# A scan, attention-like blocks and a two-layer GELU network on one core: weight quarters loaded in turns, decay rows in four blocks, a new order of steps

## The chip, the cores and the metric

The kernel runs on one core of one Trainium2 chip. The metric is the device time of one execution in microseconds; three runs were made, and the median counts. All times below that are not called a run's are from one profiled execution, counted from the start of its span. The engines are PE (matmuls; its weight loads are shown as PEld), DVE (VectorE), ACT (ScalarE), POOL (GpSimd) and SP, which issues DMAs here.

## The reference

The first part is a linear recurrence over the sequence, in chunks (a state space model), for 4 batches, 8 heads, 768 positions, 32 channels (D) and a state of 16 (N). The second part is a two-layer network on the 3072 rows of 256 that come out:

```python
log_a = np.log(np.clip(a, 1e-06, 1.0))
for c in range(nc):                       # chunks of 32
    cum = np.cumsum(la, axis=-1)
    L = np.exp(cum[..., :, None] - cum[..., None, :]) * causal
    M = np.einsum('bhin,bhjn->bhij', Cc, Bc) * L
    y = einsum('bhij,bhjd->bhid', M, xc) + einsum('bhin,bhnd->bhid', Cc, state) * np.exp(cum)
    state = exp(sum(la)) * state + sum over j of B_j x_j * exp(cum_last - cum_j)
...
h = y_rows @ w_in                         # 3072 x 256 by 256 x 2048
g = 0.5 * h * (1.0 + np.tanh(c * (h + 0.044715 * h * h * h)))
out = g @ w_out                           # 2048 x 256
```

## The kernel before, in words

**Tiles.** The kernel takes chunks of 128 positions: 6 a batch, 24 in all. Two chunks are a unit, so there are 12 units of 256 rows. The decay factors are products of `a` within a chunk; they are put into B and C (`mul`: C divided by, B multiplied with the factor), so that the block of weights of a chunk is a masked product of C and B.

**Steps of a unit u.** `G.u` multiplies C and B of the unit's two chunks into four PSUM banks (`ga` and `gb` are two each; 8 short matmuls); `M.u.0` and `M.u.1` (DVE) mask the two halves with the triangle and write them out as bf16. `D.u` makes the chunk's own addition to the state, `S.u.k` adds it to the old state, `SP.c` spreads the state of chunk c over heads. `Y.u` multiplies masked weights with x and C with the old state into the bank `yb`, and `yev.u` copies that into `xm`, the input of the network. `s1.u.i` (8 a unit, 4 matmuls of 256 columns each, L717) is the first layer, into one of two PSUM buffers `hp`; `gelu.u.i` (ACT, L721) empties it into `gT`. `s2.c.q` (4 a chunk, 4 matmuls of 256 columns, L735) is the second layer, summed over q in a bank `o_ps` (or, near the end, `yb`), emptied by `oev.c` and written out by `store.c`. Step q of `s2` needs GELUs 2q and 2q+1 and quarter q of w_out.

**Batch 0** is done in a shorter way. Its first four chunks have their own rows of a (`load_aq`, `clipq`, `Rq` the scan, `tpq` the transpose, `recip0`), and `mulc`, `mulb`, `tw` (transposes on PE), `ew` (their copies out of PSUM). x comes in by `load_x4`, is cast by `x4.k` (tile `x4b`), and `XX.u` and `XD.u` bring it into order and form the state's addition on PE; `xn.c` copies it out. Chunks 4 and 5 have `mul1`, `T1`, `ce1`, `bh1`, `N1`, `bn1`. For unit 0, `GE.2`, `GE.3` (ACT) and `ME.2`, `ME.3` (POOL) do the second half of M.

**Other batches.** `load_bc.b.i` brings in C and B. Batch 1 turns them on PE (`T.1.i`, copies `E.1.i`, then `F.1`, `N.1`, `bn.1`); batches 2 and 3 by a scratch tensor in DRAM and a transposing DMA (`load_wr`, `load_tr`, `load_bn`). `castx.u` casts x of units 2 and on. The decay factors of all batches come from two blocks of 32 rows with half a sequence each, `a_t` [64, 384]: `clip`, `R` (scan), then `tp6.0` to `tp6.3` and `tp2` (four calls) turn them by 32 rows at a time, `recip` and `recip1` invert, and `pe`, `pp`, `pend` make the factor of a whole chunk.

**Weights.** w_in and w_out come in as four quarters each (`load_wi.q`, `load_wo.q`, 512 KB, tile `wf`) and are cast in halves (`wi.q.k`, `wo.q.k`) by POOL, ACT or DVE.

**The order.** The string `ORDERED` lists all steps by hand; a step is recorded when its name comes up, on its own engine or on the one named behind the colon (`:D`, `:A`, `:P`). Each engine works through its list in order, and semaphores make it wait for data and for a buffer to be free. `~n` is n blocks of 128 columns of filler matmuls on zeros (into `yb`), `+10` is such filler ahead of an `s1` step; they are no part of the result. All large loads are issued by SP, the rows of `a` in part by ACT. A DMA that uses the same completion counter as the one eight places earlier waits for that one to land. The pools that matter: two buffers `hp`, one `o_ps`, one `yb`, eight for weight quarters, six for x.

```python
ORDERED = """
load_aq.0 load_aq.1 load_aq.2 load_aq.3 c_wz load_bc0.1 c_ident c_m4 c_sel c_tri c_zero load_bc0.0
c_unp load_a.0:A clipq load_x4 Rq tpq recip0 c_cz mulc.0 ~59 tw.1 load_wi.0 c_warm load_a.1:A
...
"""
```

Of the kernel before, what the change touches and what calls it, by code (L numbers as in the profile page):

```python
# [8 lines left out]
FP32 = mybir.dt.float32  # L9
# [8 lines left out]
load_aq.0 load_aq.1 load_aq.2 load_aq.3 c_wz load_bc0.1 c_ident c_m4 c_sel c_tri c_zero load_bc0.0  # L18
c_unp load_a.0:A clipq load_x4 Rq tpq recip0 c_cz mulc.0 ~59 tw.1 load_wi.0 c_warm load_a.1:A
ew.1.1:A mulc.1 c_bmask c_m8 tw.2 mulb ~4 tw.0 peq ew.0.2:A clip ew.0.1 load_wi.1 ew.0.0:A ew.1.2  # L20
c_par ~2 G.0 x4.1 ew.1.0 M.0.0 ~1 ppq GE.2 pendq x4.0:P XX.0 ME.2 XD.0 GE.3 xn.1 ME.3 xn.0:D
load_wi.2 SP.0 ~17 Y.0 wi.0.1:A wi.0.0:A S.0.0 yev.0.0.2 wi.1.1 XX.1 wi.1.0:A R XD.1 S.0.1
load_wi.3 S.1.0 s1.0.0 SP.1 xn.2 load_bc1.1 wi.2.0 gelu.0.0 G.1 s1.0.1 s1.0.2 M.1.1 M.1.0
load_bc1.0 load_wo.0 wi.3.0:D gelu.0.1 wi.2.1 s1.0.3 load_x.2 SP.2 pe wi.3.1 gelu.0.2 load_bc.1.1
gelu.0.3 tp6.2 s1.0.4 load_bc.1.0 gelu.0.4 load_x.3 load_wo.1 xn.3 s1.0.5 s1.0.6 Y.1 gelu.0.5 pp
tp2 gelu.0.6 tp6.3 recip1 s1.0.7 S.1.1 yev.1.0.2 mul1.0:P mul1.1:P tp6.1 pend gelu.0.7 s1.1.0
wo.0.1 T1.0 s1.1.1 T1.1 gelu.1.0 bh1 N1 gelu.1.1 s1.1.2 tp6.0 s1.1.3+10 bn1 ce1.1 load_wo.2
castx.2.None SP.3 wo.0.0 ce1.0 gelu.1.2 gelu.1.3 G.2 s1.1.4 recip.1.4 s1.1.5 gelu.1.4 M.2.1
mul.1.1:P s2.0.0.0.o D.2 M.2.0 load_x.4 gelu.1.5 s2.0.1.0.o s1.1.6 T.1.1 gelu.1.6 S.2.0 s1.1.7
SP.4 Y.2 mul.1.0 yev.2.0.2:D gelu.1.7 wo.1.0 wo.1.1 T.1.0 E.1.1:A castx.3.None:A s1.2.0 wo.2.0  # L30
s1.2.1 E.1.0 wo.2.1 load_wo.3 load_bc.2.1 N.1 gelu.2.0 F.1 s1.2.2 bn.1:D G.3 gelu.2.1 gelu.2.2 D.3
s1.2.3 s2.0.0.1.o S.3.0 S.3.1 load_bc.2.0 gelu.2.3 s1.2.4 M.3.1 s2.0.1.1.o s1.2.5 SP.6 gelu.2.4
s1.2.6 M.3.0 gelu.2.5 wo.3.0:D gelu.2.6 s2.0.0.2.o castx.4.None s1.2.7 Y.3 gelu.2.7 wo.3.1:D
s2.0.1.2.o S.4.0 yev.3.0.2 S.4.1 s2.0.0.3.o oev.0 load_x.5 s1.3.0 s1.3.1 mul.2.1 s2.0.1.3.o
load_wr.2.1 load_x.6 gelu.3.0 gelu.3.1 s1.3.2 oev.1:D SP.8 s1.3.3 s2.1.0.0.o gelu.3.2 M.4.0
# [50 lines left out]
def kernel(  # L86
# [14 lines left out]
    Q = 128  # L101
# [882 lines left out]
```

## Time and profile before

| | |
|---|---|
| runs | 118.29 us median of 3 (118.04 to 118.46) |
| the profiled execution | span 116.9 us; its own time outside of the span isn't recorded, and the median run is 1.4 us above the span |
| busy in the span | PE 110.1 (94%), ACT 72.1 (62%), DVE 69.4 (59%), POOL 21.4 (18%) |
| matmuls of the first layer (L717) | 384, 53.3 us of rows; 4 of them are issued in 0.437 us |
| matmuls of the second layer (L735) | 384 in two groups, 47.3 and 4.6 us of rows, at the same pace |
| GELU (L721, ACT) | 96, 596 ns each |
| first L717, last L735 | 12.50, 113.87 us |
| DMA | 16 MB; queue busy nearly all the time to 32 us |
| granted TensorE clock | 1.00 throughout |

Rows of PE overlap: a matmul's row lasts longer than the step to the next matmul. What it costs is the step, so the chain that ended last, which counts only steps, gives 0.437 us for four matmuls of 256 columns. In a row of the timeline the first number is the start, the second how long the group lasted, and the bracket at the end is the idle time before it with what ended that. A DMA's issue row is not its transfer; the list of DMA issues gives the time from issue to landing. In the chain, PE has 75% of the span, and DMA and SP's queue 14%, these two all before 16.7 us.

### The profile page before, as it was taken

What the parts mean: (1) busy time and instruction counts of PE and PEld (TensorE: products, weight loads), DVE (VectorE), ACT (ScalarE), POOL (GpSimd) and SP (SyncE); (2) the same over time, 40 slices, a digit from 0 to 9 for tenths busy, and PEclk for the clock granted to TensorE, in tenths of its full rate; (3) what the DMA queues carried; (4) which work ended last, traced back from release to release, by engine and by line L of the source; (5) the groups of instructions that cost most, each with busy time, mean ns of one, the idle gap of its engine ahead of it and who ended that gap; (6) DMA issues with size and microseconds to landing.
All of it is one profiled execution on the core that took longest, in us unless ns stands there. A gap on an engine that the chain in (4) does not pass through costs nothing.

```text
span 116.9 us, 3379 instructions
## 1 busy us (share of the span) xinstructions
PE 110.1 (94%) x1426; PEld 92.0 (79%) x1426; DVE 69.4 (59%) x140; ACT 72.1 (62%) x139; POOL 21.4 (18%) x38
## 2 busy tenths in 40 slices
PE   6988999998899999999999999999999999999990
PEld 2354676776789979989898999889798998999970
DVE  5898899899785936716695583049493462101020
ACT  2249899968486459565766677828465587447501
POOL 7606816908206000052200000000000000000000
PEclk9999999999999999999999999999999999999999
DMA  0999997999983929998407472044201201101113
GB/s 26 228 332 357 281 252 178 208 288 257 305 143 90 185 47 219 213 253 200 72 25 171 121 163 63 0 140 98 40 6 63 71 0 52 43 0 50 45 47 132
DMA packets 43007, 15.97 MB, mean 137 GB/s; under 512 B 36657, under 2 KB 41457, under 8 KB 42993
## 3 DMA queue, kind: packets, MB, share of 16 engines
q1 hardware_dynamic: 42800, 15.64, 56.0%
q8 instruction: 11, 0.18, 0.6%
q10 hardware_dynamic: 192, 0.13, 0.5%
q14 instruction: 4, 0.02, 0.1%
HBM read 11.04 MB, written 3.93 MB: 128 GB/s over the span
## 4 chain that ended last, share of the span: by engine, by line
PE 75%; DMA 8%; DVE 6%; SPq 6%; issue 2%; POOL 1%; ACT 0%; DVEq 0%; POOLq 0%
PE o_ps L735 33%; PE hp L717 30%; DMA bcf<-in_B_dram 8%; PE yb L735 3%; SPq L190 3%; PE ga L603 3%; PE yb L658 2%; DVE m L613 2%; PE yb L667 2%; DVE ce L523 1%; SPq L150 1%; DVE bh L327 1%; DVE bc L484 1%; SPq L159 1%; SPq L183 1%
## 5 line engine op out<-in xcount | busy, mean ns | idle before, releaser
L721 ACT ACTIVATE gT<-hp 128x512 bf16<-128x512 f32 x96 | 54.3, 596 | 25.0 <-PE hp L717 24.6
L717 PE MATMUL hp<-xm,w_in_sb 128*128 128x256 bf16 x384 | 53.3, 273 | 0.6 <-ACT gT L721 0.4
L735 PE MATMUL o_ps<-w_out_sb,gT 128*128 128x256 bf16 x352 | 47.3, 273 | 0.0
L717 PEld LDWEIGHTS <-w_in_sb 128*128 128x128 bf16 x384 | 41.4, 114 | 3.5 <-issue 1.9
L735 PEld LDWEIGHTS <-gT 128*128 128x128 bf16 x384 | 37.0, 98 | 4.9 <-issue 1.1
L327 DVE COPY o_sb<-o_ps 128x256 f32<-128x256 f32 x13 | 5.5, 425 | 23.8 <-PE o_ps L735 20.4
L613 DVE TENSOR_TENSOR m<-ga,tri 128x1024 bf16<-128x1024 f32 x12 | 14.6, 1218 | 0.1
L613 DVE TENSOR_TENSOR m<-gb,tri 128x1024 bf16<-128x1024 f32 x11 | 13.4, 1219 | 0.7 <-PE gb L603 0.7
L323 ACT ACTIVATE o_sb<-o_ps 128x256 f32<-128x256 f32 x9 | 3.5, 385 | 9.2 <-PE o_ps L735 9.2
L705 PE MATMUL yb<-wz 128*128 128x512 bf16 (+3 forms) x23 | 7.6, 481 | 1.1 <-DVE wz L220 1.1
L691 DVE SCALAR_TENSOR_TENSOR sp_new<-s_new,pend,bmask 128x256 bf16<-128x256 f32 x17 | 7.9, 476 | 0.0
L327 DVE CAST xm<-yb 128x512 bf16<-128x512 f32 x6 | 4.1, 687 | 5.8 <-PE hp L636 4.8
L684 DVE SCALAR_TENSOR_TENSOR s_new<-s_new,pend,hp 128x64 f32<-128x64 f32 x13 | 3.6, 279 | 6.4 <-PE hp L636 6.2
L705 PEld LDWEIGHTS <-wz 128*128 128x128 bf16 x26 | 3.0, 120 | 5.1 <-issue 3.2
L667 PE MATMUL yb<-m,x 128*32 128x128 bf16 x192 | 6.1, 220 | 0.0
L603 PE MATMUL ga<-ce,bh 32*128 32x256 bf16 x48 | 4.7, 273 | 1.3 <-DVE bn L327 0.9
L484 POOL TENSOR_TENSOR bc<-bc_t,pt 128x768 bf16<-128x768 f32 x2 | 3.0, 1494 | 13.8 <-DMA bc_t<-in_C_dram 13.7
L658 PE MATMUL yb<-ce,sp_new 128*32 128x128 bf16 x160 | 5.3, 221 | 0.0
L603 PE MATMUL gb<-ce,bh 32*128 32x256 bf16 x48 | 4.7, 273 | 0.0
L735 PE MATMUL yb<-w_out_sb,gT 128*128 128x256 bf16 x32 | 4.6, 273 | 0.0
L667 PEld LDWEIGHTS <-x 128*32 128x32 bf16 x192 | 3.8, 97 | 0.8 <-issue 0.8
L323 ACT ACTIVATE xm<-yb 128x512 bf16<-128x512 f32 x6 | 3.6, 595 | 1.1 <-PE hp L636 1.1
(115 smaller groups left out, 79.5 us busy)
## 6 DMA issues: line engine op xcount, KB each, us to landing
out_dram<-o_sb SPq DMA_DIRECT2D x24, 128.0 KB, 1.9
x_t<-in_x_dram SPq DMA_DIRECT2D x20, 128.0 KB, 3.9
wf<-in_moe_w_in_dram SPq DMA_DIRECT2D x4, 512.0 KB, 6.7
wf<-in_moe_w_out_dram SPq DMA_DIRECT2D x4, 512.0 KB, 5.5
bc_t<-in_C_dram SPq DMA_DIRECT2D x3, 384.0 KB, 5.8
bc_t<-in_B_dram SPq DMA_DIRECT2D x3, 384.0 KB, 5.5
scr<-bc SPq DMA_DIRECT2D x4, 192.0 KB, 2.2
x_t<-in_x_dram SPq DMA_DIRECT2D x1, 512.0 KB, 5.8
```

Source lines behind the costliest of these rows:

```text
L323: nc.scalar.activation(o, i, AF.Copy)
L327: nc.vector.tensor_copy(out=o, in_=i)
L484: (nc.gpsimd if eng == "POOL" else nc.vector).tensor_tensor(out=d["bc16"][:, i], in0=d["bc"].rearrange("p i h (r n) -> p i r h n", r=R6)[: ...
L603: nc.tensor.matmul(out=gbank(g)[:, 256 * k:256 * k + 256], lhsT=bh_of(2 * u + k)[gs], rhs=ce_of(2 * u + k)[gs], start=True, stop=True, til ...
L613: nc.vector.tensor_tensor(out=m_of(u)[:, 2 * i:2 * i + 2].rearrange("p g k e t -> p (g k e) t"), in0=gx[i].rearrange("p g (k t) -> p (g k) ...
L658: nc.tensor.matmul(out=y4[32 * j:32 * j + 32, k, w], lhsT=sp[:, 32 * h:32 * h + 32], rhs=ce_of(gc)[:, h % 2], start=first(j), stop=False, ...
L667: nc.tensor.matmul(out=y4[32 * j:32 * j + 32, k, w], lhsT=X16[u][:, k, 32 * h:32 * h + 32], rhs=m[:, h // 2, h % 2, :], start=first(j), st ...
L691: nc.vector.scalar_tensor_tensor(out=sp_new.rearrange("p (g d) -> p g d", g=4), in0=(XN[0][:, H * D:H * D + 64] if gc == 0 else state[("s" ...
L705: nc.tensor.matmul(out=t[:, 0:m * 128], lhsT=wz, rhs=w3.to_broadcast([128, m, 128]), start=True, stop=True, skip_group_check=True)
L717: nc.tensor.matmul(out=hp[:, j * T:(j + 1) * T], lhsT=w_in_k[:, w, q, k], rhs=xm[:, w, u * T:(u + 1) * T], start=(w == 0), stop=(w == 1))
L721: nc.scalar.activation(gts[u][:, 2 * i:2 * i + 2], hps.pop((u, i)).rearrange("p (j t) -> p j t", j=2), AF.Gelu_apprx_tanh)
L735: nc.tensor.matmul(out=ops[gc], lhsT=gts[u][:, fi, k * Q:(k + 1) * Q], rhs=w_out_sb[:, fi, :], start=(fi == 0 and (u > 0 or k == 0)), stop ...
```

## The change

The order of steps is new throughout. What else changes:

- **Loads.** `load_aq` is one DMA of 128 rows in place of four. `a_t` has 128 partitions: four blocks of 32 rows, each with a quarter of the sequence (192 columns) and, beside it, rows for chunks 4 and 5; `load_a` are four DMAs, all issued by ACT. `load_x.u.k` are the two halves of `load_x.u`. SP's order of loads begins now: C, B, wi.1, x4, wi.0, wo.0, bc1 (B), wi.2, bc1 (C), wi.3, wo.1, half of x.2, wo.2, the other half, B and C of batch 1, wo.3, x.3, x.4.
- **Decay rows.** `tp6` is one transpose of [128, 192] and `tp2` one of [128, 64]; `recip.b` is one step for each batch. `pe` and `pend` fit the new layout (`pend` is two copies).
- **Constants.** Parts of `c_zero`, `c_sel` and `c_unp` become steps of their own (`c_az`, `c_ends`, `c_unz`, `c_selp`, `c_sub`); in the new order `c_selp` and `c_unp` are on POOL. `c_warm`, a GELU of one column, stands behind `oev.23`.
- **Start.** `mulb` and `x4` are cut into 2 and 4 pieces. `M` of unit 0 becomes `M.0.0`, `MD.0.3` (DVE, one bank), `GE.0.2` and `ME.0.2`; unit 1 has `M.1.0`, `GE.1.2`, `GE.1.3`, `ME.1.2`, `ME.1.3`. `XX.1` and `XD.1` go into the bank pair `gb`. `G.1` stands ahead of `XD.0`, and `XD.1` behind `s1.0.1`. `Y.0` and `yev.0` are done in two halves (`Yw.0.w`).
- **Second layer of units 0 and 1.** Both chunks of a unit are done by quarters in turn, side by side in one bank: unit 0 in `o_ps` (as before), unit 1 in `yb`.

```diff
-    def load_x(u):
+    def load_x(u, k):
...
-    def load_aq(i, eng):
-        (nc.scalar if eng == "ACT" else nc.sync).dma_start(out=aq_t[32 * i:32 * i + 32], in_=a_rows(i * Q, Q))
+    def load_aq(eng):
+        dma(eng)(out=aq_t, in_=a_of(0, Q, 4, batch * H, Q))
...
+        if i == 0:
+            dma(eng)(out=a_t[0:k, 0:2 * Q], in_=a_of(0, QL, 3, batch * H, 2 * Q))
+        elif i == 1:
+            dma(eng)(out=a_t[k:, 0:QL], in_=a_of(3 * QL, 0, 1, batch * H, QL))
+        elif i == 2:
+            dma(eng)(out=a_t[0:k, 2 * Q:AL], in_=a_of(4 * Q, Q // 2, 3, batch * H, Q))
+        else:
+            dma(eng)(out=a_t[k:, 2 * Q:2 * Q + Q // 2], in_=a_of(S - Q // 2, 0, 1, batch * H, Q // 2))
...
     def f_tp2():
-        for k in range(4):
-            turn(rt0[1][32 * k:32 * k + 32], r_t[32:64, Q + 64 * k:Q + 64 * k + 64], 2)
+        turn(rt0[1], r_t[:, 2 * Q:2 * Q + Q // 2], 2)
...
-    def f_tp6(q):
-        i, j = divmod(q, 2)
-        turn(rt[32 * q:32 * q + 32], r_t[32 * i:32 * i + 32, 192 * j:192 * j + 192], R6)
+    def f_tp6():
+        turn(rt, r_t[:, 0:QL], R6)
...
-            XN[c] = pso.tile([128, 512], FP32, name="o_ps") if c in (0, 3) else psh.tile([128, 512], FP32, name="hp")
+            XN[c] = gx[1][:, k] if u else pso.tile([128, 512], FP32, name="o_ps") if k == 0 else psh.tile([128, 512], FP32, name="hp")
...
+    def f_MD(u, g):
+        nc.vector.tensor_tensor(out=m_of(u)[:, g].rearrange("p k e t -> p (k e) t"),
+                                in0=gbank(g).rearrange("p (k t) -> p k t", t=Q), in1=tri_b(4), op=ALU.mult)
...
-            if u == 0:
+            if u < 2:
                 if k == 0:
-                    ops["0"] = pso.tile([128, 512], FP32, name="o_ps")
-                ops[gc] = ops["0"][:, k * d_model:(k + 1) * d_model]
+                    ops["u"] = yb if u else pso.tile([128, 512], FP32, name="o_ps")
+                ops[gc] = ops["u"][:, k * d_model:(k + 1) * d_model]
...
-        for k, q in [(k, q) for q in range(4) for k in range(2)] if u == 0 else [(k, q) for k in range(2) for q in range(4)]:
+        for k, q in [(k, q) for q in range(4) for k in range(2)] if u < 2 else [(k, q) for k in range(2) for q in range(4)]:
```

The new order, from the first `G` to the first steps of unit 2, and its last line:

```
tw.0 ew.0.0:A ew.0.2:D ew.1.0:A ~6 G.0 R
ew.1.2 ew.1.1:A c_tri c_selp:P wi.1.0 GE.0.2 c_unp:P ~3 ppq x4.2:P load_wo.0 x4.1:P pendq x4.0 M.0.0
MD.0.3 x4.3 ME.0.2 load_bc1.0 ~23 XX.0 wi.1.1:D c_par load_wi.2 wi.0.0 pe xn.1 G.1 XD.0 GE.1.2 tp2
xn.0:D SP.0 wo.0.0 pp S.0.0 ~4 Yw.0.0 Yw.0.1 GE.1.3 wi.0.1:D yev.0.1.2 mul1.0:P S.0.1 pend
load_bc1.1 wo.0.1 XX.1 yev.0.0.1:D load_wi.3 xn.3 wi.2.1 M.1.0 s1.0.0 s1.0.1 load_wo.1 gelu.0.0
load_x.2.0 XD.1 T1.0 wi.2.0 ME.1.2 load_wo.2 S.1.0 s1.0.2 recip1 ME.1.3:D gelu.0.1 s1.0.3 mul1.1 bh1
N1 xn.2 s2.0.0.0.o S.1.1 T1.1 SP.1 SP.2 wi.3.1 ce1.1:D SP.3 load_x.2.1 gelu.0.2 s2.0.1.0.o gelu.0.3
s1.0.4 ce1.0:D wi.3.0:D s1.0.5 bn1 Y.1 gelu.0.4 G.2 wo.1.0 tp6 wo.1.1:D s1.0.6 gelu.0.5 load_bc.1.0
s1.0.7 yev.1.0.2 M.2.1 gelu.0.6 s2.0.0.1.o s2.0.1.1.o gelu.0.7 s1.1.0 s1.1.1 wo.2.1:A M.2.0 gelu.1.0
gelu.1.1 wo.2.0 s2.0.0.2.o s2.0.1.2.o castx.2.None:D D.2 s1.1.2 recip.1 S.2.0 load_bc.1.1 SP.4
...
s2.11.1.1.o store.22 s2.11.1.2.o s2.11.1.3.o oev.23 c_warm store.23
```

More of the change, by code (lines that the diff above doesn't have):

```diff
@@ L30 @@
[L30 to L35, printed above, removed]
```

318 lines of the change are left out of this document (179 added, 139 removed).

## The prediction

> **What bounds the kernel now.** I read the table of stages (busy time of each engine in stretches of the span) first, then the chain that ended last, then the timeline from 2 to 34 us.
>
> ```profile
> core 0: us, PE busy (x) PEld busy (x) DVE busy (x) ACT busy (x) POOL busy (x), PEclk, DMA share, GB/s
> 12.00:16.00 4.00, 3.56 (x65) 2.52 (x62) 3.55 (x7) 3.50 (x8) 2.62 (x4) 1.00 1.05 261
> ...
> 24.00:28.00 4.00, 3.71 (x67) 3.05 (x66) 3.96 (x7) 2.86 (x5) 1.50 (x3) 1.00 1.02 303
> 28.00:32.00 4.00, 3.11 (x43) 2.57 (x41) 3.29 (x7) 2.10 (x5) 1.57 (x3) 1.00 1.10 290
> 32.00:36.00 4.00, 4.00 (x71) 3.42 (x69) 3.62 (x7) 2.77 (x6) 0.72 (x1) 1.00 0.67 119
> 36.00:60.00 24.00, 24.00 (x327) 21.36 (x325) 14.70 (x27) 15.31 (x29) 4.01 (x4) 1.00 0.78 155
> ```
>
> PE has no idle time left from 32 us on, to the end of the matmuls at 113.9; the DMA queue is busy throughout until 32. So the end is set by when PE starts its main work and by what it loses before 32 us. The chain is matmuls one after the other from 30.26 to 113.87 (83.6 us). Before that come the losses:
>
> ```profile
> 12.50 0.60 PE L717 MATMUL hp<-xm,w_in_sb 128*128 128x256 bf16 x4
> 14.67 1.09 PE L717 MATMUL hp<-xm,w_in_sb 128*128 128x256 bf16 x8 [0.20 <-ACT gT L721]
> 15.95 1.09 PE L717 MATMUL hp<-xm,w_in_sb 128*128 128x256 bf16 x8 [0.20 <-ACT gT L721]
> 29.69 0.28 PE L603 MATMUL ga<-ce,bh 32*128 32x256 bf16 x2 [0.89 <-DVE bn L327]
> ```
>
> From 12.5 PE has only first-stage matmuls, and alternates with the GELU over two banks: two groups (0.87 us of issue) every 1.28 us. The second stage cannot fill in, because its weights come late (the wo quarters land at 18.2, 26.2, 27.6 and 30.8). Later it waits for batch 1's tiles on DVE.
>
> The ledger of 12.50 to 30.26 (17.76 us) in issue times of the chain: 19 first-stage groups and 2 second-stage ones of 4 matmuls at 0.437 (9.18); G.1 to G.3 at 0.33 (0.99); Y.1, Y.2 at 0.56 (1.12); the transposes T1, N1 (0.66) and T.1, N.1 (1.05); pp, D.2, D.3 (0.52). That is 13.5, so 4.25 us are idle or filler (`s1.1.3+10`). This is all that the change can win after the first s1.
>
> **Part 1: the start.** The first s1 follows XX.0, XD.0, xn.0, SP.0, Y.0, yev.0, and XX.0 follows the load of x.
>
> ```profile
> 8.65 0.63 ACT L323 ACTIVATE x4b<-x_t 128x512 bf16<-128x512 f32 x1 [0.30 <-DMA x_t<-in_x_dram]
> 8.69 0.61 POOL L325 CAST x4b<-x_t 128x512 bf16<-128x512 f32 x1 [3.53 <-DMA x_t<-in_x_dram]
> ...
> 9.35 0.27 PE L571 MATMUL o_ps<-x4b,unp 32*128 32x256 bf16 x1 [0.48 <-POOL x4b L325]
> ```
>
> The a rows come in one DMA, C and B are issued at 0.81 instead of 1.73, and the constants leave DVE (POOL copies selp and unp). DVE started clipq at 4.25 though the rows had landed at 3.24, so the decay chain moves ahead by about 1 us, and G.0 from 8.13 to about 7.6, since it now also waits for half of mulb on POOL. None of it counts while XX.0 waits for x; without that cover it would be worth the 0.5 us of G.0. SP issues wi.1 before x4. With the landings of before (C 3.5 us after issue, B 1.14 later, 512 KB of w_in 1.42, x4 2.2) C lands at 4.35, B at 5.5, wi.1 at 6.9, x4 at 9.1 (8.63 before). The casts take 0.6 to 0.7 on POOL and ACT. POOL's queue before them now holds some 13 more short instructions and wi.1.0, and I put its end at 9.2 to 9.6: its memsets and copies go by the rows from 0.81 to 5.16 (0.2 to 0.9 each), and one cast is stretched as w_in's was beside the scan (1.04 against 0.61). XX.0 then starts at 10.0 to 10.2, 0.75 later. XD.0 now stands behind G.1 (0.33) and behind xn.1, which ACT must read out of the same bank: 11.2 to 11.5. Then xn.0 (0.34), SP.0 (0.4), Y (0.45), and on DVE S.0.0, wi.0.1 (0.42) and S.0.1 before yev's half (0.35). First s1 at **13.5, against 12.50: +1.0**. Bounds: +0.7 if POOL keeps up, +1.8 if the scan (0.94) stops it for its whole length.
>
> **Part 2: a second table load on ACT.** The new order has c_warm, the first GELU, at its end. The list of ACT's instructions then shows a table load before the first copy, which is free, and a second one between xn.3 and gelu.0.0.
>
> ```profile
> 2.21 1.28 ACT L231 ACT_TABLE_LOAD   x1 [2.21 <-issue]
> ...
> 3.50 0.20 ACT L231 ACTIVATE warm<-warm 128x1 f32<-128x1 f32 x1
> ```
>
> xn.3 (after XX.1) ends at 13.8, the load at 15.1; without it gelu.0.0 would start at 14.2, when s1.0.0 is through. PE meanwhile does s1.0.0, s1.0.1, XD.1 (0.38), T1.0 (0.22) until 15.0, then waits for the bank of gelu.0.0 until 15.7: 0.7 us lost. I take the row's 1.28.
>
> **Part 3: PE from there.** In the new order quarters of s2.0, XD.1, T1 and N1 stand between the s1 groups, so that PE no longer waits for GELUs (0.49 apart): from 15.1 to 32 ACT has 19 GELUs and 7 other pieces, 12.4 of 17 us. Whether the quarters are there in time goes by the queue, with the same increments (bc1 1.2, wo 1.5, x 0.5 a half, bc_t 2.1). Landing, then ready after its cast or multiply, then PE's need by issue times in order:
> wi.2 14.6, 15.8, 18.0. wi.3 17.2, 18.9, 19.7. wo.1 18.7, 19.9, 20.6. wo.2 20.7, 21.9, 22.3. C and B of batch 1 25.4, 26.9, 28.6. wo.3 26.9 (30.8 before: 432 KB less stand ahead of it), 28.6, 29.8.
> All in time by 0.4 to 2.2 us. SP's waits in this list are for loads eight places back, landed by then. A late wo.3 would hold ACT too: wo.3.0 stands there before gelu.2.0.
>
> DVE: six transposes (1.94) and two (1.07) become two (0.25 and 0.55); one reciprocal of 1.03 becomes three of about 0.35. This takes away the 3.6 us for which POOL's bc0s waited on rt, part of the chain of before. M.1.1 (1.22) becomes two copies on ACT (0.58 each), a select on POOL (0.61) and a multiply on DVE (at most 0.61). The next wait is D.3: after T.1.1 at 28.8 DVE does E.1.1 (0.96), bn (0.54), F (1.44), castx.3 (0.34), so 32.1 and 32.2 with the hand-over, and PE is there at 31.8: 0.4 lost. Then Y.3 needs the bank that s2.1 now fills, free after oev.3, and M.3.0 behind it on DVE: 36.9 to 37.3 against PE's 37.2. I take nothing and leave 0.5 in the range. Loads of x by halves are the same DMAs; the stores and scratch transposes have over 2 us to spare at Y.5.
>
> **Sum.** First s1 +1.0. Lost time 4.25 less (0.7 + 0.4): -3.1. G.1 and pp (0.53) go ahead of the first s1, XD.1 (0.38) behind it: -0.15. Together **-2.25**, the last matmul at 111.6, the span 114.65. The 1.4 us between this span and the median run lie around it and stay: 118.29 - 2.25 = 116.0. Own range 115.3 to 117.3: -0.3 (POOL) and -0.4 (load half hidden) below, +0.8 (POOL) and +0.5 (Y.3) above.
>
> **Rivals.** *A switch of tables with running work costs more than the row.* The row of before has nothing ahead of it on ACT, and its next instruction starts 0.01 us after it; here it follows copies. If the switch lasts twice the row, gelu.0.0 moves from 15.1 to 16.4 and PE, without other work there, loses 1.3 more: 117.3, still faster. Chance 0.12. [...]
>
> *The DMA queue holds PE: slower.* PE works in order, and s2.0.*.3 stands before s1.2.1. If wo.3 lands later than 29.2, with 0.6 for the cast, each us costs one; from 31.4 the gain is gone. For it: the queue is never idle, the two quarters of bc1 took 2.4 us for 256 KB, and four loads from ACT's queue now share the start. At a pace 20% lower than before's it lands at 32.1, giving 116.0 + 2.9 = 118.9. Against it: fewer bytes stand ahead, and before moved 7072 KB by 30.8. Chance 0.15.
>
> *The new order gives the gain back after 32 us.* Before has no idle there; here s2.1 holds yb until oev.3, and M.3.0 waits behind it. A stall of 1.1 us for each of Y.3 and Y.4 (an M each) would give 118.2. DVE's 3.62 busy of 4 at 32 to 36 speaks for it, the other 60 us against it. Chance 0.10.
>
> *The load hides and POOL keeps up:* 116.0 - 0.7 - 0.3 = 115.0. Chance 0.08.
>
> **How the numbers follow.** Forecast 0.55, the others as given. Measurement can tell about 0.3%, 0.35 us. Faster: 0.55 + 0.12 + 0.08 + 0.03 of the third; same 0.05; slower 0.15 + 0.02. Range 115.0 to 117.9: from the best case past the switch rival, short of the slower one and of part of the third.
>
> **What would show it.** Right: two ACT_TABLE_LOAD rows, the second ending near 15.1; XX.0 near 10.1, first s1 near 13.5; no wait of PE for GELU of over 0.2 us between 16 and 30; PE busy 4.00 of 4 from 33 on; last matmul near 111.6. Wrong: x4b waiting for POOL beyond 10.5, a GELU starting after 16, PE waiting on a w_out_sb cast near 20 to 30, or idle at Y.3.

## The result, and the profile after

The changed kernel takes 123.62 us (median of 4 runs, 123.17 to 124.66) against 118.38 for the kernel before (118.04 to 118.62) on the same chip: a ratio of 1.044, 95% interval 1.037 to 1.051. The forecast was 116.0, faster. The profiled execution has a span of 122.9 us against 116.9; it is the slowest of the four, two others have 121.4 and 121.5. Here and below the medians count all runs, while the ratios leave out runs that are more than 1.5% above the fastest of the same kernel.

The table of stages, as read for the prediction (busy time of each engine in stretches of the span; after the five engines' numbers the granted clock of PE, the DMA share and GB/s):

```profile
core 0: us, PE busy (x) PEld busy (x) DVE busy (x) ACT busy (x) POOL busy (x), PEclk, DMA share, GB/s
...
8.00:12.00 4.00, 0.73 (x8) 0.35 (x6) 0.44 (x3) 0.97 (x3) 1.26 (x5) 0.98 1.08 308
12.00:16.00 4.00, 3.62 (x17) 1.42 (x16) 3.96 (x9) 2.04 (x6) 2.69 (x5) 0.50 0.85 217
16.00:20.00 4.00, 4.00 (x80) 2.44 (x81) 1.90 (x7) 1.67 (x4) 3.47 (x7) 0.50 0.95 276
20.00:24.00 4.00, 3.74 (x58) 2.48 (x55) 2.60 (x6) 3.55 (x10) 0.68 (x2) 0.74 1.15 274
24.00:28.00 4.00, 3.92 (x70) 3.25 (x69) 3.88 (x10) 3.17 (x8) 0.75 (x1) 1.00 0.84 247
28.00:32.00 4.00, 4.00 (x48) 3.38 (x49) 3.73 (x6) 2.93 (x6) 1.15 (x1) 1.00 0.88 127
32.00:36.00 4.00, 3.59 (x62) 3.09 (x55) 3.24 (x4) 2.86 (x6) 2.23 (x3) 1.00 1.16 235
36.00:60.00 24.00, 23.94 (x303) 21.36 (x300) 15.65 (x28) 16.60 (x32) 2.47 (x3) 1.00 0.63 123
```

From 8 to 12 no engine is busy for more than 1.26 of 4 us, while the DMA queue is full (share 1.08), and from 12 to 20 PE runs at half its clock, where the profile before has 1.00 throughout. From 24 to 36 PE loses 0.49 us in all (0.08, 0.00, 0.41), where before it lost 1.18 (0.29, 0.89, 0.00). The chain that ended last names what the start waits for (start, length, what):

```profile
4.00 7.50 DMA a_t<-in_a_dram
...
12.38 0.40 PE ga L634 x2
...
13.64 2.47 PE yb L744 x6
16.12 0.32 PE o_ps L602
...
19.74 0.98 PE gb L602 x8
...
21.15 1.28 ACT L760
22.45 1.09 ACT gT L760 x2
```

7.5 us of it are the smallest load of all, 8 KB of `a` (`load_a.3`). The engines' timelines say who waits (idle time and releaser in brackets), and SP's list of waits says when x was issued:

```profile
11.63 0.36 DVE L368 TENSOR_SCALAR ac<-a_t 128x384 f32<-128x384 f32 x1 [3.56 <-DMA a_t<-in_a_dram]
11.91 0.42 DVE L358 COPY ce<-hp 128x256 bf16<-128x256 bf16 x1
```

```profile
12.38 0.40 PE L634 MATMUL ga<-ce,bh 32*128 32x256 bf16 x2 [3.64 <-DVE ce L358]
...
13.50 2.61 PE L744 MATMUL yb<-wz 128*128 128x512 bf16 x6
16.05 0.39 PE L602 MATMUL o_ps<-x4b,unp 32*128 32x256 bf16 x1
```

```profile
12.79 0.94 POOL L356 CAST x4b<-x_t 128x256 bf16<-128x256 f32 x2 [3.06 <-DMA x_t<-in_x_dram]
```

```profile
SPq L156 <- DMA a_t<-in_a_dram: 2.0, 1, 2.0
SPq L199 <- DMA aq_t<-in_a_dram: 2.0, 1, 2.0
...
SPq L206 <- DMA a_t<-in_a_dram: 1.6, 1, 1.6
```

In the new order `clip` (L368) stands on DVE ahead of `ew.0.2`, the copy of `ce` that G.0 needs. So G.0 waits for the last row of a_t, though it has no use for a_t: 12.38 against 8.13. x is issued at 4.96 (2.81 before), because its counter is that of the decay rows, and lands at 12.73 (8.63). The two other waits of SP are of the same kind: batch 0's last B (L156) and the third quarter of w_in (L206) are issued only when loads of a_t have landed. The filler ahead of XX.0 then runs at half clock (2.61 us for six matmuls of 512 columns, at 0.50). XX.0 starts at 16.05 (9.35), the first s1 at 20.69 (12.50). The 8.19 us between these two are +4.25 up to G.0, +2.45 from G.0 to XX.0 and +1.49 from XX.0 to the first s1. From the first s1 to the last second-stage matmul it is the other way round: 99.14 us against 101.37, with the last matmul at 119.83.

**Why 8 KB take 7.5 us.** The trace has each step of a DMA's completion counter. Each load of 32 rows there makes 16 steps as its parts land (a.3 from 6.33 to 11.51). The decay rows, now four blocks in one DMA, make five: one at 2.08 and four at 4.77 to 4.94 (before, the last of their four DMAs landed at 3.24). The two loads of three blocks (a.2 and a.0) make four, the last three of them at 8.08, 8.29, 9.31 and at 9.66, 9.95, 11.28. Of a.3's 16 parts 13 had landed at 7.65, the last three at 9.93, 10.21 and 11.51; of x's, 13 at 10.03, the last three at 11.69, 11.87 and 12.73. So three parts of each of these two were late, as many as the blocks of the slow loads a.2 and a.0. Which DMA engines carried these parts, the steps don't tell. That the blocks of the slow loads held them is the likely reading; it is not shown. The prediction took the merged decay rows to land no later than before and did not price the other loads of `a`.

### The profile page after: what moved, and what is told of

Same layout as the page of the kernel before. It is cut to its first block, busy times and chain, and to the rows that moved or that the text cites. A ratio compares the mean times of both kernels' runs of the same rounds, so it can differ in the third digit from the quotient of the medians.

```text
span 122.9 us, 3384 instructions
## 1 busy us (share of the span) xinstructions
PE 112.7 (92%) x1422; PEld 93.5 (76%) x1422; DVE 68.3 (56%) x135; ACT 73.3 (60%) x141; POOL 21.7 (18%) x51
## 4 chain that ended last, share of the span: by engine, by line
PE 78%; DMA 6%; DVE 5%; ACT 4%; ACTq 3%; issue 1%; DVEq 0%
PE hp L756 31%; PE o_ps L774 27%; DMA a_t<-in_a_dram 6%; PE yb L774 5%; PE ga L634 3%; PE yb L744 3%; PE yb L703 3%; DVE sp_new L730 2%; PE yb L694 2%; ACT gT L760 1%; ACT x L354 1%; ACT L760 1%; DVE m L644 1%; ACTq L167 1%; PE gb L602 1%
## 5 line engine op out<-in xcount | busy, mean ns | idle before, releaser
L774 PE MATMUL o_ps<-w_out_sb,gT 128*128 128x256 bf16 x320 | 44.1, 273 | 0.0
L644 DVE TENSOR_TENSOR m<-gb,tri 128x1024 bf16<-128x1024 f32 x10 | 12.1, 1215 | 0.0
L744 PE MATMUL yb<-wz 128*128 128x512 bf16 (+2 forms) x22 | 8.9, 557 | 1.1 <-DVE wz L237 1.1
L730 DVE SCALAR_TENSOR_TENSOR sp_new<-s_new,pend,bmask 128x256 bf16<-128x256 f32 x17 | 9.0, 544 | 0.1
L774 PE MATMUL yb<-w_out_sb,gT 128*128 128x256 bf16 x64 | 8.8, 273 | 0.0
L354 ACT ACTIVATE xm<-yb 128x512 bf16<-128x512 f32 (+1 forms) x11 | 6.3, 577 | 2.3 <-PE yb L703 1.6
L356 POOL CAST x<-x_t 128x512 bf16<-128x512 f32 x3 | 1.8, 612 | 30.7 <-ACT o_sb L354 12.2
L634 PEld LDWEIGHTS <-bh 32*128 32x128 bf16 x96 | 1.9, 95 | 4.9 <-issue 3.4
L694 PEld LDWEIGHTS <-sp_new 128*32 128x32 bf16 x160 | 3.0, 97 | 2.2 <-issue 1.6
```

The costliest lines, as they stand in the source:

```text
L354: nc.scalar.activation(o, i, AF.Copy)
L634: nc.tensor.matmul(out=gbank(g)[:, 256 * k:256 * k + 256], lhsT=bh_of(2 * u + k)[gs], rhs=ce_of(2 * u + k)[gs], start=True, stop=True, til ...
L644: nc.vector.tensor_tensor(out=m_of(u)[:, 2 * i:2 * i + 2].rearrange("p g k e t -> p (g k e) t"), in0=gx[i].rearrange("p g (k t) -> p (g k) ...
L694: nc.tensor.matmul(out=y4[32 * j:32 * j + 32, k, w], lhsT=sp[:, 32 * h:32 * h + 32], rhs=ce_of(gc)[:, h % 2], start=first(j), stop=False, ...
L730: (nc.gpsimd if eng == "POOL" else nc.vector).scalar_tensor_tensor(out=sp_new.rearrange("p (g d) -> p g d", g=4), in0=(XN[0][:, H * D:H * ...
L744: nc.tensor.matmul(out=t[:, 0:m * 128], lhsT=wz, rhs=w3.to_broadcast([128, m, 128]), start=True, stop=True, skip_group_check=True)
```

## The experiments

Each is compared with runs of the kernel before on the same chip (medians 118.2 to 118.9). "Start" is G.0, XX.0 and the first s1; the changed kernel has 12.38, 16.05, 20.69. Two theories stood against each other at first: A, the a rows' loads are slow by their shape; B, x and the last rows are late behind the second quarter of w_in and by SP's counters.

**a rows by blocks.** In `load_aq` and `load_a`, one DMA for each block of 32 rows (seven DMAs more):

```diff
-        dma(eng)(out=aq_t, in_=a_of(0, Q, 4, batch * H, Q))
+        for j in range(4):
+            (nc.scalar, nc.sync)[j % 2].dma_start(out=aq_t[32 * j:32 * j + 32], in_=a_of(j * Q, 0, 1, batch * H, Q))
...   # the same for the two loads of three blocks
```

> The changed kernel with the rows of a loaded by one DMA for each block of 32 rows (aq four, a.0 and a.2 three each; 8 DMAs more), as the kernel before does it; nothing else differs. [...] Theory B (the rows come late because C, B and a quarter of w_in, 1 MB, stand ahead of them on the same engines): a_t at 10 us or later, first s1 after 19, time over 122.

123.24 us, ratio 1.043 (1.039 to 1.047): no gain, where 116 to 117.8 was expected if A alone held the start. The decay rows were there at 3.26 and the blocks of a_t by 7.18, but a.3, issued at 5.24, landed at 9.66, behind w_in's quarter (9.49), and x, issued at 6.21, at 12.48. Start 10.76, 14.43, 19.07. A alone falls; once the shape is mended, B holds the start.

**More filler.** 72 further blocks of filler ahead of G.0.

```diff
-... ew.0.2:D ew.1.0:A ~6 G.0 R
+... ew.0.2:D ew.1.0:A ~78 G.0 R
```

> The changed kernel with 72 blocks of filler matmuls more (18 of 512 columns) ahead of G.0, so that PE works through the gap from 8.5 to 12.4 us; nothing else differs. If the clock falls to a half because PE was idle, it stays at 1.00; the filler ahead of XX.0 then takes 1.3 us and not 2.6, XX.0 starts near 14.6 (with x4b) and not at 16.05, first s1 near 18.0 and not 20.7, time near 121.0. If the clock falls for another reason (the late start as such, or power), it falls in spite of the filler, and the time stays at 123 to 124.

121.94, ratio 1.034 (1.028 to 1.040). Two of its runs kept the full clock throughout; the start was 12.40, 14.38, 18.22 in the profiled one. G.0 starts where it did, and 0.010 of the ratio, 1.2 us, are won. The profiled run was at half clock for 3.4 us, from about its first s1 on. The two runs at full clock, 121.65 and 121.70, are 1.029 times the kernel before, so that the half clock by itself costs nearly 1.8 us of the changed kernel's 5.2.

**One table load.** `c_warm` (the first GELU) behind `load_a.3` instead of at the end of the list.

```diff
-mulb.0:P tw.2 mulb.1 tw.1 load_a.3 clip load_wi.0 ...
+mulb.0:P tw.2 mulb.1 tw.1 load_a.3 c_warm clip load_wi.0 ...
...
-... oev.23 c_warm store.23
+... oev.23 store.23
```

> The changed kernel with c_warm behind load_a.3, so that the GELU table is loaded once, in ACT's idle time; nothing else differs. By the row (1.28 us, the GELU 0.02 us behind it) gelu.0.0 starts 0.9 us earlier, bounded by s1.0.0, and the time falls by 0.7 to 0.9 us to about 122.8. If a switch has a price beyond its row, it falls by 2 us or more. If the table load is hidden by the half-speed matmuls, it stays at 123.6.

122.32, ratio 1.035 (1.030 to 1.039). The profiled run has one table load and 0.63 instead of 1.76 us from s1.0.0 to gelu.0.0. But its first s1 also comes 1.28 us earlier (19.41; a_t landed earlier and the half clock was shorter), and from there to the last second-stage matmul it needs 99.15 us against 99.14. So nothing of the gain in these two profiles can be put down to the table.

**Only a_t by blocks.** As the first, with the decay rows left in one DMA.

> The changed kernel with a.0 and a.2 by one DMA for each block of 32 rows, and aq still by one DMA of four blocks. Theory A: a_t at 7 to 9 us, x4 still held until aq has landed near 4.9 (its issue waits for aq's counter) and landed near 10, first s1 at 14 to 15.5, clock 1.00, time 116.5 to 118.5: nearly all of the loss is a_t's. If instead aq's lateness were the main thing, G.0 would stay near 12 and the time over 122.

122.25 median, one run at 119.53 and three near 122.3, so that no interval can be given. Start 11.05, 14.72, 18.56; a.3 landed at 10.13, x at 10.64.

**x ahead of w_in.** The second quarter of w_in behind x and a.3 on SP, its cast on POOL behind x's.

```diff
-... load_bc0.0 load_wi.1 peq c_m16 c_cz c_ends load_x4 mulc.1 mulc.0
-mulb.0:P tw.2 mulb.1 tw.1 load_a.3 clip load_wi.0 ...
+... load_bc0.0 peq c_m16 c_cz c_ends load_x4 mulc.1 mulc.0
+mulb.0:P tw.2 mulb.1 tw.1 load_a.3 clip load_wi.1 load_wi.0 ...
```

> The changed kernel with one load moved: the second quarter of w_in (512 KB) is issued by SP behind x and the last a row, not ahead of them, and its cast on POOL is moved behind x's casts so that it doesn't hold them. Nothing else differs. Theory (the 8.2 us lost before the first s1 come from a_t's last rows and x landing behind that quarter, and from x's issue waiting for a counter): a_t lands by about 8.5, x by 8 to 9.5 (it still waits for the decay rows' counter until 5.0, so perhaps 9.5), clip ends by 9, G.0 near 9.5, XX.0 at 10 to 11.5, first s1 at 13.5 to 15, the clock stays at 1.00 or falls in one window at most, time 116.5 to 118.5. Rival (the loads are slow because of their shape, several blocks in one DMA, wherever they stand): a_t still lands at 11 or later, G.0 at 12, the first s1 at 18 or later, time 122 or more.

123.33, ratio 1.039 (1.035 to 1.044). x was issued at 1.94 and landed at 8.48, yet a.3 landed at 10.69, its last three parts at 10.03 to 10.69, when a.0's landed (9.82 to 10.50). Start 11.55, 15.22, 19.48. The rival was right: B alone falls too. The start waits for two loads at once, and each edit mended one.

**The same, one table.**

> As the run with x ahead of the second quarter of w_in, and besides the first use of the GELU table stands behind load_a.3, ahead of ACT's other work, so that ACT loads a table once only. If the second table load costs what the prediction took (0.7 us on the path, between xn.3 and the first GELU), this is 0.4 to 1.0 us faster than that run; s1.0.0 to gelu.0.0 falls from 1.76 to about 0.6. Rival (PE has other work beside that load once the clock is full): no difference beyond 0.3 us. If theory holds in both, time 115.5 to 117.8, which would beat the kernel before.

122.74, ratio 1.035 (1.029 to 1.042), not told apart from the run before it; 98.81 from the first s1 on against 99.01.

**clip late.** `clip` and `R` behind MD.0.3 on DVE, loads as changed.

```diff
-mulb.0:P tw.2 mulb.1 tw.1 load_a.3 clip load_wi.0 ... ~6 G.0 R
+mulb.0:P tw.2 mulb.1 tw.1 load_a.3 load_wi.0 ... ~6 G.0
...
-MD.0.3 x4.3 ME.0.2 ...
+MD.0.3 x4.3 clip R ME.0.2 ...
```

> The changed kernel with the clip of a_t and its row reductions moved behind MD.0.3 on DVE, so that ew.0.2 (the last copy that G.0 needs) doesn't stand behind the wait for a_t. Loads as changed. If clip's wait alone holds G.0: G.0 starts near 8 to 9 instead of 12.4, PE doesn't idle for 3.6 us, the clock stays at 1.00 for longer; XX.0 still waits for x (landing 12.7) and starts at 14 to 15 instead of 16.05, and with a full clock the rest of the start takes 1 us less: first s1 17 to 18.5, time 120.5 to 122.5. If the place of clip doesn't matter since x is late anyway and the clock falls in another idle window before x: XX.0 at 15 to 16, time 123 or more.

122.04, ratio 1.029 (1.025 to 1.033). G.0 starts at 9.18, as forecast, and XX.0 at 12.31, the first s1 only at 17.71. The clock fell to half all the same (a mean of 0.957 in the profiled run), and PE waited 1.21 us for `pe`, which on DVE stands behind clip (11.64), the scan and a cast of w_in. Clip's place on DVE is worth 1.8 us of the ratio.

**Kernel before, decay rows by one DMA.** The four loads of `aq_t` as one of four blocks, nothing else.

```diff
-(nc.scalar if eng == "ACT" else nc.sync).dma_start(out=aq_t[32 * i:32 * i + 32], in_=a_rows(i * Q, Q))
+if i == 0:
+    nc.scalar.dma_start(out=aq_t, in_=bass.AP(tensor=a.tensor, offset=a.offset, ap=[[Q, 4], [S, batch * H], [1, Q]]))
```

> The kernel before with one part of the change alone: the decay rows of the four blocks are loaded by one DMA instead of four (the order stays). Prediction's view (fewer DMAs, rows there sooner or no later): time 118.0 to 118.4, no difference. Rival (the one DMA of four blocks lands at 5 instead of 3.2, as in the changed kernel): clipq starts at 5.0 instead of 4.25, G.0 at about 8.5, XX.0 stays at 9.35 since x is what it waits for there: 118.1 to 118.8, at most 0.5 slower.

The four runs spread from 121.18 to 125.79 (median 124.46), and no interval can be given, but the fastest is 2.3 us above the median of the kernel before (118.85). In the profiled one, the fastest:

```profile
9.45 0.35 DVE L338 TENSOR_SCALAR ac<-a_t 64x384 f32<-64x384 f32 x1 [1.66 <-DMA a_t<-in_a_dram]
9.72 0.41 DVE L328 COPY ce<-hp 128x256 bf16<-128x256 bf16 x1
```

The decay rows landed at 4.59, and clipq hardly suffered (4.61 against 4.25). But ACT's next load, the second half of a_t, waits for their counter: issued at 4.61 instead of 3.15, landed at 9.42 instead of 6.97. clip waits for it and G.0 for clip: 10.19 against 8.13, first s1 14.23 against 12.50. Both views had looked at clipq alone, and the expected 0.5 was too small.

**Both mended.** The edits of "a rows by blocks" and "x ahead of w_in" together (where the a rows go by blocks, the further lines of code make line numbers three higher).

> The changed kernel with both causes taken away at once: the a rows come by one DMA for each 32-row block (eight more DMAs), and x and the last a row are issued ahead of the second quarter of w_in. Each alone left the other wait standing (a_t 9.9 with x at 12.5; x at 8.5 with a_t at 10.7). Theory (two loads in a row of AND, each enough to hold the start): a_t lands by 7.5 to 8.3, x by 8 to 9, G.0 at 8.3 to 9, XX.0 at 9.5 to 10.5, first s1 at 13 to 14, the clock at 0.99 or more, the second table load costs 0.7, time 116.5 to 118. If the start is near 13.5 and the time is 118.5 or more, the second half of the prediction (2.2 to 3.2 won from the first s1 on) is wrong. Rival (eight more DMAs shift the waits to other counters): x or a_t still beyond 10, time 120 or more.

120.20, ratio 1.015 (1.008 to 1.023): 0.029 of the ratio, 3.4 us, come back, where either edit alone gave 0.1 to 0.6. a.3 lands at 8.58, x at 8.98, the parts of each now within 0.5 us of each other. The start is 9.55, 12.99, 16.83, later than expected; clip still stands in the way:

```profile
8.80 0.36 DVE L371 TENSOR_SCALAR ac<-a_t 128x384 f32<-128x384 f32 x1 [2.27 <-DMA a_t<-in_a_dram]
9.08 0.42 DVE L361 COPY ce<-hp 128x256 bf16<-128x256 bf16 x1
```

PE idles 1.76 us and its clock is at half from 9.27 to 12.69. Behind the first s1 it has the full clock throughout, and needs 97.91 us to the last second-stage matmul, 3.46 less than before.

**Both mended, one table,** and the same once more with C, B and x named ahead of the a rows in the list.

> The run with both causes taken away, and besides the first use of the GELU table behind load_a.3 on ACT, so that the table is loaded once. 0.4 to 1.0 faster than that run: 115.8 to 117.3, which beats the kernel before by 1 to 2 us. If PE has other work during the second load, no difference beyond 0.3 us.

> The run with both causes taken away and one table, with C, B and x moved ahead of all a rows but the decay rows on SP's list, so that x is among the first eight loads and waits for no counter (issued at about 2.8 instead of 4.8). x lands at 8 to 8.6, as before the change, the a pieces 0.5 later than in the run with both: if x's landing sets XX.0 there, XX.0 moves to 9.4 and the time falls by 0 to 0.7 us against that run; if a_t through clip sets it, it gets 0 to 0.8 slower.

121.09 (ratio 1.026, 1.018 to 1.034) and 120.27 (1.015, 1.009 to 1.022). The second edit left the order of every engine's instructions, and the counters, as they were, so the two are one program measured twice; nothing follows on x. They show the scatter: the profiled spans are 119.8 and 118.2, at mean clocks of 0.969 and 0.986. Against the run with two tables no gain shows.

**x first, clip late,** the a rows still in DMAs of three and four blocks.

> The a rows stay in the DMAs of several blocks, as changed; x ahead of the second quarter of w_in, and clip with its reductions behind MD.0.3 on DVE, so that neither x nor the wait for a_t stands ahead of G.0, M.0.0 and XX.0. If only those two waits hold the start (and not the slow a rows by themselves): G.0 near 9, XX.0 near 9.5 to 11 (x lands at 8.5), but the scan and pe, which XD.0 and SP.0 need, follow clip at about 11.7 and end near 14, so first s1 at 15.5 to 16.5, clock 0.97 or more, time 119 to 120.5. If a_t is needed as late as that, it is as slow as with x late: 122.

120.92, ratio 1.016 (1.009 to 1.024), start 8.77, 10.92, 16.13, near what was expected: with both waits out of the way of G.0 and XX.0, `pe` holds the first s1: on DVE it stands behind M.0.0, MD.0.3, clip (11.01), the scan and a cast of w_in, and starts at 13.10.

**Start in place.** Both mended, a.3 issued first of ACT's a rows, clip behind `ew.0.2`; and the same with one table.

```diff
-c_wz load_aq c_az load_a.1 c_ident ...
+c_wz load_aq c_az load_a.3 load_a.1 c_ident ...
...
-mulb.0:P tw.2 mulb.1 tw.1 load_a.3 clip load_wi.1 load_wi.0 ... ew.0.2:D ew.1.0:A ~6 G.0 R
+mulb.0:P tw.2 mulb.1 tw.1 load_wi.1 load_wi.0 ... ew.0.2:D clip ew.1.0:A ~6 G.0 R
```

> The run with both causes taken away, and besides: the last a row (8 KB) is issued first of the a rows on ACT instead of last, and clip stands behind ew.0.2 on DVE instead of ahead of it. Theory (what is left of the lost start is clip's wait ahead of G.0, and the half clock that the idle PE brings): a_t lands by 7.5, clip at 8.0 to 8.4 without a wait, G.0 at 8.0 to 8.6, PE idles under 1 us, clock 0.99 or more, XX.0 at 10 to 10.6, first s1 at 13.2 to 14, last second-stage matmul at 111.5 to 113.5, time 116 to 118 (the forecast was 116.0 with first s1 at 13.5). If first s1 is there by 14 and the time is 119 or more, the second half of the forecast falls as well. Rival (something else holds the start, the order of ACT's or POOL's copies): XX.0 beyond 11.5, time 119 or more.

> As the run with the start in place, with the GELU table loaded once, ahead of ACT's work. If the second load lies on the path with the price forecast: 0.5 to 0.9 faster, 115.3 to 117.3, the fastest of all. If not: within 0.3 us of that run.

121.80 (ratio 1.028, 1.024 to 1.033) and 121.05 (1.013, 1.005 to 1.021). G.0 at 7.9 and XX.0 at 10.8 and 10.5 were as expected, the first s1 was not: 16.85 and 16.77. The cast of w_in's second quarter was still in its old place on DVE, ahead of `pe`, and that quarter, put behind x, landed at 12.8 and 12.7; PE had less work (2.59 and 2.37 of 4 us busy from 12 to 16) and dropped to half clock at 13.6 and 13.7. The run with one table has a median that is 0.75 us lower, about what was expected, but behind the first s1 its profile is no shorter (99.93 us against 99.58), and its six runs also had more clock (a mean of 0.980 against 0.973, about 0.8 us of 120), so that nothing can be put down to the table. A load that is moved without the in-order step that waits for it moves the wait.

**Kernel before, w_in ahead of x.** One swap in SP's list:

```diff
-c_unp load_a.0:A clipq load_x4 Rq tpq recip0 c_cz mulc.0 ~59 tw.1 load_wi.0 c_warm load_a.1:A
+c_unp load_a.0:A clipq Rq tpq recip0 c_cz mulc.0 ~59 tw.1 load_wi.0 load_x4 c_warm load_a.1:A
```

> The kernel before with one part of the change alone: the first quarter of w_in (512 KB) is issued by SP ahead of x instead of behind it. Theory (loads that stand together are served together, and x waits for a counter too): x lands at 9.9 to 11 instead of 8.6, XX.0 at 10.6 to 11.8 instead of 9.35, clip's rows 0.5 to 1 us later too, PE idle before XX.0 with perhaps a window at half clock; 119.3 to 121. The prediction's view (increments by bytes in order: x 0.5 us later, half hidden): 118.3 to 118.9.

124.66, ratio 1.053 (1.047 to 1.059), more than the whole change costs, and beyond both views. Its stages and POOL's cast of x:

```profile
8.00:12.00 4.00, 0.74 (x11) 0.52 (x11) 2.37 (x6) 0.46 (x3) 0.07 (x1) 1.00 0.93 287
12.00:16.00 4.00, 3.41 (x53) 1.47 (x57) 1.93 (x4) 2.98 (x7) 3.46 (x6) 0.50 0.89 257
16.00:20.00 4.00, 4.00 (x79) 2.09 (x72) 1.53 (x5) 2.09 (x4) 1.19 (x2) 0.50 0.87 212
```

```profile
11.93 0.61 POOL L325 CAST x4b<-x_t 128x512 bf16<-128x512 f32 x1 [6.75 <-DMA x_t<-in_x_dram]
```

x is issued at 3.45 instead of 2.81, and lands at 11.87 instead of 8.63. XX.0 is 3.24 us late. PE stood idle for 2.69 us ahead of it and then ran at half clock, and from XX.0 to the first s1 (17.89 against 12.50) it needs 2.15 us more. The picture is that of the changed kernel, without its a rows.

**Loads in the order of need.** The a rows by blocks with a.3 first; `c_warm` on ACT ahead of a.2 and a.0, by which x gets an early counter; then w_in's first quarter, which s1.0.0 needs, then the second, with its casts behind yev; clip and R behind MD.0.3. Against the run with both mended:

```diff
-c_wz load_aq c_az load_a.1 c_ident load_a.2 ...
+c_wz load_aq c_az load_a.3 load_a.1 c_warm c_ident load_a.2 ...
...
-mulb.0:P tw.2 mulb.1 tw.1 load_a.3 clip load_wi.1 load_wi.0 ... ~6 G.0 R
+mulb.0:P tw.2 mulb.1 tw.1 load_wi.0 load_wi.1 ... ~6 G.0
...
-MD.0.3 x4.3 ME.0.2 load_bc1.0 ~23 XX.0 wi.1.1:D c_par load_wi.2 wi.1.0 wi.0.0 pe ...
+MD.0.3 x4.3 clip R ME.0.2 load_bc1.0 ~23 XX.0 c_par load_wi.2 wi.0.0 pe ...
...
-load_bc1.1 wo.0.1 XX.1 yev.0.0.1:D load_wi.3 ...
+wi.1.0 load_bc1.1 wo.0.1 XX.1 yev.0.0.1:D wi.1.1:D load_wi.3 ...
```

> The changed kernel with its loads in the order of need: a rows by one DMA for each block, the small last row first; the first use of the GELU table on ACT ahead of the a rows' other loads, so that x takes over an early counter and is issued near 3; then the first quarter of w_in (which s1.0.0 needs), then the second, with its casts behind yev and ahead of s1.0.2; clip and its reductions behind MD.0.3. Forecast by theory (the start was all that failed; 97.9 us from the first s1 to the last second-stage matmul, as in the run with both causes taken away): x lands at 8 to 8.7, G.0 at 8 to 8.6, XX.0 at 9.5 to 10.3, pe at 12, first s1 at 13.7 to 14.8, clock 0.99 or more, last second-stage matmul at 111.6 to 112.8, time 116.0 to 117.4, below the kernel before. Rival (PE's idle time ahead of Y still brings the half clock, or the first quarter of w_in lands beyond 13): first s1 beyond 15.5, time 118.5 or more.

119.72 median (118.18 to 122.50), ratio 1.007 (1.003 to 1.011). In the profiled run (118.43) the clock is full all the time and the start is 8.14, 10.28, 14.80:

```profile
8.00:12.00 4.00, 3.41 (x65) 1.75 (x65) 3.32 (x5) 3.13 (x11) 2.49 (x8) 1.00 1.05 254
12.00:16.00 4.00, 3.01 (x75) 2.08 (x75) 3.64 (x14) 1.78 (x7) 1.67 (x3) 1.00 1.08 324
16.00:20.00 4.00, 3.34 (x56) 2.91 (x38) 3.34 (x9) 2.83 (x8) 3.52 (x6) 1.00 1.06 330
20.00:24.00 4.00, 3.49 (x64) 2.94 (x64) 4.00 (x8) 2.93 (x7) 1.40 (x3) 1.00 1.11 252
```

From the first s1 it needs 98.74 us, 0.8 more than with both mended; the last second-stage matmul ends at 113.54 against 113.87 before. Ten of the twelve runs have a mean clock of 0.97 to 0.99 and are slower.

**a rows by two queues.** Three of the a loads go by SP, all a rows land before x, clip and the scan stand in DVE's idle time ahead of M.0.0.

```diff
-c_wz load_aq c_az load_a.3 load_a.1 c_warm c_ident load_a.2 ...
-load_bc0.1 c_bmask c_unz load_a.0 load_bc0.0 peq ...
+c_wz load_aq c_az load_bc0.1 load_a.3 load_a.1 c_ident ...
+load_bc0.0 load_a.2:S c_bmask c_unz load_a.0 peq ...
...   # c_warm back behind tw.1; clip R behind ew.0.2:D; wi.0.1 on POOL behind wi.0.0
```

> The run with the loads in the order of need, with these edits: three of the a-row loads go by SP between B and x, three by ACT, so that all a rows land before x; clip and the scan stand behind ew.0.2, in DVE's idle time ahead of M.0.0; both halves of the first w_in quarter's cast on POOL. If a_t's late rows (9.6) held the rest of the start: a_t lands by 7.3, scan by 8.7, x at 9.0 to 9.5, XX.0 near 10.3, pe by 11.5, first s1 at 13.3 to 14.0, time 116.0 to 117.4, the fastest of all. If x (0.7 to 1 us later than there) or the casts of the first w_in quarter hold it: first s1 at 14.3 or later, time 117.8 to 119.5, and the change's loads have no better arrangement among those tried.

119.17 (118.56 to 120.38), ratio 1.007 (1.004 to 1.010). a_t landed by 7.23, x at 9.37, and the first s1 came at 14.14, the earliest of all with the change. But PE then needed 101.07 us. Its waits between 14 and 36 us (who waits for whom, us in total, times, longest):

```profile
PE ga L486 <- POOL bc0s L478: 0.8, 1, 0.8
PE hp L674 <- DVE x L361: 0.7, 1, 0.7
PE hp L759 <- ACT bh L357: 0.5, 1, 0.5
PE hp L759 <- DVE xm L361: 0.4, 1, 0.4
```

and from 16 to 20 the clock was 0.60 (at half from 16.84 to 20.25). So no version tried beats the kernel before.

## Why the prediction was wrong, step by step

**Part 1, the start: this step failed.** "None of it counts while XX.0 waits for x" took x to be the only wait of the start, and "C lands at 4.35, B at 5.5, wi.1 at 6.9, x4 at 9.1" was worked out by bytes in the order of issue. C and B came as forecast (4.2 and 5.9), wi.1 at 8.4, x at 12.7. Three things were left out. First, the loads of `a`: neither the a_t loads nor the wait of `clip` for them, which stands on DVE ahead of a copy that G.0 needs, were followed at all, and the merged decay rows were taken to land no later than the four DMAs. They landed at 4.94 instead of 3.24, so that the decay chain, which "moves ahead by about 1 us" in the prediction, began later: clipq went from 4.25 to 4.96. G.0 came at 12.38 where 7.6 was forecast. Second, "SP's waits in this list are for loads eight places back, landed by then" did not hold for x: eight places back stood the slow decay rows, and it waited 2.0 us for them. Third, an idle PE was taken to cost its idle time, and here it cost clock besides (nearly 1.8 us, by the run with more filler). POOL's queue, on which the range hung ("+0.7 if POOL keeps up"), was not the limit: POOL stood idle for 3.06 us ahead of its first cast of x. Both mended loads together give 3.4 us back, the order of need another 1.0; the swap of x and w_in alone makes the kernel before 6.2 us slower. For the start +1.0 was forecast and +8.2 measured. At best 14.14 was reached for the first s1, still 1.6 us behind the kernel before; what holds this rest is not shown.

**The rival of the DMA queue** had the right cause at the wrong place. It looked for a late wo.3; that quarter landed at 29.1, earlier than before (30.8). The queue held the start, where the prediction had only asked for the order of bytes.

**Part 2, the second table load: the row was right, the loss was not found.** The load takes 1.28 us at 21.15 and the first GELU starts 0.02 after it:

```profile
21.15 1.28 ACT L760 ACT_TABLE_LOAD   x1
22.45 1.09 ACT L760 ACTIVATE gT<-hp 128x512 bf16<-128x512 f32 x2
```

So the rival of the table switch fell: ACT's copy ahead of the load ends 0.02 us before it (20.75, 0.38 long), and no time beyond the row shows on either side. That a switch could last twice its row was an assumption of the author; no run shows it. But a loss of 0.7 us doesn't show either. In four pairs of profiles with two loads and with one, the time from the first s1 to the last second-stage matmul is 99.14 and 99.15, 99.01 and 98.81, 97.91 and 98.09 (the repeat at the same clock), 99.58 and 99.93: within 0.4 both ways. Three of the pairs differ in half clock behind the first s1 (1.37 us against none, 3.41 against 1.45, 3.53 against 3.80), mostly to the favour of one load, so that this hides no gain of it. The medians of the runs don't settle it: with one load they are 1.3, 0.6 and 0.75 us lower in three pairs, and 0.9 and 0.1 higher in the fourth and its repeat. That PE catches the load up in later waits is a likely reason; it was not tested.

**Part 3, the gain behind the first s1: right in size, and the waits agree, but it is not free of the start.** 3.25 was forecast (3.1 and 0.15). The changed kernel gained 2.23 with 1.37 us of half clock behind its first s1, worth 0.7 (an estimate: half of it); at full clock (both mended) it was 3.46. PE waited for a GELU for 0.3 us in all from 14 to 36. The 0.4 put down to D.3 came, at another place: Y.2 waited 0.4 for the spread of the state on DVE. Nothing was given back after 32 us: 23.94 of 24 busy from 36 to 60, so that rival fell. What the sum had wrong is that it adds. The 97.91 belong to a first s1 at 16.83. With the first s1 at 14.80 it was 98.74, also at full clock. At 14.14 it was 101.07; 3.4 us of that were at half clock, worth 1.7 by the same estimate, which leaves some 99.4. PE's waits from 14 to 36 grew from 1.1 us (both mended) to 1.4 and 2.4, at 14.14 for batch 0's last B and C among others. So "all in time by 0.4 to 2.2 us" seems to have held because the late start gave the loads time; that is the likely reading of three profiles, no experiment on it alone. The forecast's 13.5 plus 97.9 was reached by no run, and the best last matmul (113.54) is 0.3 us ahead of the kernel before. One term was taken over too simply: the 1.4 us around the span compare a median with another execution. In single executions they are 2.0 for the kernel before (118.10 and 116.1) and 1.8 for the changed one (124.66 and 122.9), too little to matter here.

**What stays open:** how much of the scatter among runs of one program is the stretches at half clock alone, what holds the start between 12.50 and 14.14, and whether a start near 13.5 is to be had with another set of loads.

## What to carry to other kernels

Before relying on merged loads, measure when one lands: the same bytes landed 1.7 to 4.1 us later here in one DMA of three or four blocks than block by block (4.94 against 3.26, 9.31 against 6.37, 11.28 against 7.18, where nothing else was changed), and the last parts of the loads behind them were late too. For each load that moves, write down what its issue waits for, and which in-order step waits for its landing and what stands behind that step; mending one of two such waits can show next to nothing (0.1 and 0.6 us here, against 3.4 for both). Where a change leaves PE idle, price the clock too (nearly 1.8 us here), and don't add a gain behind a stage to a shift of that stage when both draw on the same DMA queue.

## What the runs showed of the hardware

**The clock.** After one idle stretch of 3.64 us PE's clock was at half for 10.24 us (11.82 to 22.06), though PE was busy for 3.62 and 4.00 of 4 us in it; with 1.76 us idle (both mended) it fell for 3.4 us. How long PE must idle isn't told by these runs: 2.04 us ahead of G.0 left the full clock in the kernel before with its decay rows by one DMA, and with more filler it fell at 18.18, in an idle stretch of only 0.40. Every stretch of half clock ahead of the last matmul lasted 3.41 us or two, three or four times that (6.83, 10.24, 13.65). Mean clocks of whole runs mostly came in steps: 1.00, 0.986, 0.972, 0.958, each about 3.4 us more of half clock in a span of 120 (an estimate: twice 0.014 of the span). Why the clock stayed at half for 10.24 us with PE busy, and why it fell after 1.76 us idle here and not after 2.04 there, is not shown.

**A full DMA queue.** With the queue full (a DMA share of 0.84 to 1.21 in stretches of 4 us from 4 to 32) the 512 KB quarters landed 4.7 to 7.6 us after their issue before the change and 4.8 to 9.3 us after it, and the 8 KB of a.3 took 7.5. So the bytes of a load alone didn't tell here when it lands; its place in the queue (x in the kernel before at 8.63, and at 11.87 behind w_in's first quarter) and the shape of the loads (the two of three blocks at 9.31 and 11.28, by blocks at 6.37 and 7.18) counted for more.
